# A PReLU gate's second projection by seven products for eight, its first projection in one PSUM bank, and weight forms written out once and read back

## The chip, the cores and the metric

The kernel runs on one core of one Trainium2 chip. A core has a matrix engine (TensorE, PE in the profile), a vector engine (VectorE, DVE), an activation engine (ScalarE, ACT), a general engine (GpSimd, POOL) and a queue engine that issues transfers (SyncE, SP). On-chip working memory is SBUF, with 128 partitions. Matmuls write into PSUM, which this kernel uses as eight banks of 512 float32 numbers for each partition; DVE and ACT read results from there. The metric is the device time of one execution in microseconds (us), as the median of several runs.

## The reference

Three stages follow one another; the output of one is the input of the next.

```python
A, Bm, C = softmax-like blocks of q, k and 32 landmark means        # 4 batches x 8 heads x 576 x 64
for _ in range(6): Z = 2 * Z - Z @ Bm @ Z                            # 32 x 32 pseudo-inverse
x = A @ Z @ C @ v                                                    # becomes 2304 x 512
h = x @ w_in;  x = (h * np.cos(h)) @ w_out                           # first gate, 512 -> 2048 -> 512
h = x @ w_in2; g = np.maximum(h, 0) + alpha * np.minimum(h, 0)       # second gate, 512 -> 2048
out = g @ w_out2                                                     # 2048 -> 512, float32, 2304 rows
```

The weights are given as float64. All else is float32.

## The kernel before, in words

**Precision.** A float32 matrix product is made of three matmuls. Each operand is split into a rounded high part and a low remainder (`hi` by ACT, `lo` by a subtraction on DVE or POOL), and the products hi·hi, hi·lo and lo·hi are added up in PSUM. The float64 weights are turned into float32 on the chip by three bit operations of DVE per 256 numbers (`convert`), and are written to DRAM tensors (`wi2d` and `wo2d` for the second gate) from which later stages load them.

**The second gate.** The change touches this gate alone, and what feeds it. Its 2304 tokens are worked off in chunks: chunks 0 to 3 of 512 tokens, chunk 4 of 256. Each chunk has eight steps, which I call ticks; a tick takes 256 of the 2048 hidden columns. Two ticks share a weight block (`sg`, four of them), and odd chunks take the blocks in reverse order, so that three block changes fall into each chunk. In the trace, ticks 1 to 8 of chunk 0 run from about 404 to 486 us, chunks 1 to 3 from 486 to 738 us, and chunk 4 to about 796 us.

**First projection of a tick** (`strassen`, L1341 to L1387). A product of two 2 x 2 block matrices is made by seven block products in place of eight, with sums of blocks on either side (the list `PRODUCTS`). A block product is six matmuls of 256 columns (two steps of 128 in depth, three matmuls each). The results are added up in four 256-wide quarters of two PSUM banks, `h` and `x`. Between the products, ACT or DVE copies a quarter out (L391, L393: `keep`), so that the next product can start there from zero, and at the end DVE adds both banks to the copies (L1383: `cross`, 512 elements each). The left operands, called forms here, are A11, A12, A21, A22 and the sums S1 to S4 of the weights, each split in hi and lo. S1 to S4 of all blocks are made once in chunk 0 and stay in SBUF (16 places `sr`); A11, A12 and A22 are loaded from `wi2d` (L1211) and split again for every block in every chunk (4 places `ss`). The right operands (B11, T1 and so on, made in `y_load`) belong to the chunk.

**PReLU and second projection of a tick.** DVE makes alpha·min(h, 0) (L1424) and adds max(h, 0) (L1427), for two halves of 512 elements. ACT makes the high part (L1429), DVE or POOL the low part (L396, a helper's line that many places share). Then come 24 matmuls of 512 columns (L1441): two halves by four groups of 128 tokens by three matmuls, adding up over the eight ticks in four PSUM banks `acc`. At a chunk's end the banks are copied out (L1461) and stored (L1467).

**What sets the order.** Every operation is named (`b25:9` is the ninth operation of the tick 25), and a long string `ORDER` lists the names in the order in which the program issues them; `Plan.go` (L313) walks it. An ending /V, /A or /G puts an operation on DVE, ACT or POOL where it may run on several. Each engine works its own operations off in that order. Buffers are places that rotate (`place`): an operation that fills one waits for the last reader of what was there before. Eight of the 16 blocks of w_out2 are converted under the first gate; the other eight in chunk 0 of the second gate (`late_wo2`, L1296).

## Time and profile before

| what | value |
|---|---|
| three runs, us | 801.34, 803.44, 803.97 |
| median, us | 803.44 |
| the profiled execution: its own time, us | 802.37 |
| its span in the trace, us | 800.6 |
| busy share of PE, DVE, ACT, POOL | 98%, 74%, 50%, 26% |
| granted clock of TensorE, mean over the span | 1.000 |
| data moved by DMA | 103.34 MB |

The span is the time between the first and the last instruction of the trace; the execution's own time is a little longer. A share of busy time is a mean over stages with different limits, so each stage has to be read by itself. Times in the trace count from the span's start.

### The profile page before, as it was taken

The numbers are of one execution on the slowest core, as the hardware profiler recorded it, in microseconds if no ns is written. First come the engines' busy times: TensorE is split into PE (matmuls) and PEld (weight loads), VectorE is DVE, ScalarE is ACT, GpSimd is POOL, SyncE is SP. The second block draws the span as 40 slices with busy tenths as digits, with TensorE's granted clock in tenths as the row PEclk, the third lists the DMA queues.
The fourth block names the chain that finished last, engine by engine and source line by source line (L and its number), as shares of the span: only waits on it lengthen the run. The fifth ranks groups of instructions, "written<-read, shape, count | busy, mean of one in ns | idle before, by whom it ended". The sixth has DMA issues, their size and how long they took to land.

```text
span 800.6 us, 16949 instructions
## 1 busy us (share of the span) xinstructions
PE 784.7 (98%) x6546; PEld 702.9 (88%) x6546; DVE 594.9 (74%) x1246; ACT 403.2 (50%) x919; POOL 209.0 (26%) x227
## 2 busy tenths in 40 slices
...
GB/s 259 259 296 138 120 191 187 151 203 179 223 167 264 119 265 112 237 166 109 198 93 122 89 97 93 80 27 41 53 79 40 54 38 95 47 46 33 83 84 26
DMA packets 106208, 103.34 MB, mean 129 GB/s; under 512 B 54160, under 2 KB 81296, under 8 KB 106128
## 3 DMA queue, kind: packets, MB, share of 16 engines
...
HBM read 79.96 MB, written 22.28 MB: 128 GB/s over the span
## 4 chain that ended last, share of the span: by engine, by line
PE 80%; DVE 8%; DMA 5%; ACT 3%; issue 2%; SPq 2%; POOL 1%; DVEq 0%; ACTq 0%
PE acc L1441 23%; PE acc L1071 20%; PE h L1360 11%; PE h L1046 10%; PE x L1360 8%; PE x L1002 2%; DVE m L396 2%; DMA m<-in_moe_w_in_dram 2%; DMA m<-in_moe_w_out_dram 1%; DMA m<-wi2d 1%; PE x L1405 1%; PE h L1405 1%; SPq L547 1%; PE x L939 1%; DMA wi2d<-m 1%
## 5 line engine op out<-in xcount | busy, mean ns | idle before, releaser
L396 POOL TENSOR_TENSOR m<-m,m 128x288 fp32r<-128x288 f32 (+4 forms) x156 | 150.5, 977 | 514.9 <-ACT m L1429 179.2
L1071 PE MATMUL acc<-m,m 128*128 128x288 f32 x1536 | 230.5, 297 | 0.4 <-DVE m L393 0.4
L1071 PEld LDWEIGHTS acc<-m,m 128*128 128x128 f32 x1536 | 210.5, 188 | 13.8 <-issue 7.9
L1441 PE MATMUL acc<-m,m 128*128 128x512 f32 x864 | 219.5, 394 | 1.0 <-ACT m L1429 0.9
L1441 PEld LDWEIGHTS acc<-m,m 128*128 128x128 f32 x864 | 154.0, 188 | 30.2 <-ACT m L1429 1.8
L396 DVE TENSOR_TENSOR m<-m,m 128x512 fp32r<-128x512 f32 (+4 forms) x244 | 146.0, 622 | 44.2 <-ACT m L1429 18.5
L1046 PE MATMUL h<-m,m 128*128 128x288 f32 x768 | 123.8, 298 | 0.9 <-DVE m L1056 0.4
L1046 PEld LDWEIGHTS h<-m,m 128*128 128x128 f32 x768 | 107.7, 188 | 7.1 <-DVE m L1056 3.2
L1360 PE MATMUL h<-m,m 128*128 128x256 f32 x660 | 93.3, 281 | 0.6 <-ACT m L391 0.6
L1429 ACT ACTIVATE m<-m 128x512 fp32r<-128x512 f32 (+1 forms) x80 | 46.1, 585 | 93.3 <-DVE m L1427 88.5
L1360 PEld LDWEIGHTS h<-m,m 128*128 128x128 f32 x660 | 87.9, 188 | 5.6 <-ACT m L391 1.0
L1055 ACT ACTIVATE m<-m,quarter 128x288 f32<-128x288 f32 x128 | 67.4, 533 | 37.2 <-DVE m L1053 36.6
L1360 PE MATMUL x<-m,m 128*128 128x256 f32 x576 | 81.6, 282 | 0.0
L1360 PEld LDWEIGHTS x<-m,m 128*128 128x128 f32 x576 | 76.5, 189 | 4.0
L1051 ACT ACTIVATE m<-h 128x288 int32<-128x288 f32 x128 | 51.6, 406 | 47.3 <-PE h L1046 46.6
L1056 DVE TENSOR_TENSOR m<-m,h 128x288 f32<-128x288 f32 x128 | 57.3, 451 | 22.6 <-ACT m L1055 18.1
L1053 DVE SCALAR_TENSOR_TENSOR m<-h,m 128x288 f32<-128x288 f32 x128 | 57.5, 451 | 18.0 <-ACT m L1051 17.0
L391 ACT ACTIVATE m<-h 128x256 f32<-128x256 f32 (+2 forms) x86 | 33.3, 391 | 73.3 <-PE h L1360 62.8
L1058 ACT ACTIVATE m<-m 128x288 fp32r<-128x288 f32 x128 | 54.4, 438 | 21.1 <-DVE m L1056 13.6
L1192 ACT ACTIVATE m<-m 128x512 fp32r<-128x512 f32 x68 | 41.5, 624 | 34.2 <-DMA m<-wi2d 14.2
L1427 DVE SCALAR_TENSOR_TENSOR m<-m,m 128x512 f32<-128x512 f32 x64 | 46.4, 741 | 0.8
L1383 DVE TENSOR_TENSOR m<-h,m 128x512 f32<-128x512 f32 x32 | 22.0, 686 | 32.7 <-ACT m L391 21.8
...
## 6 DMA issues: line engine op xcount, KB each, us to landing
...
m<-wi2d SPq DMA_DIRECT2D x56, 256.0 KB, 3.3
...
m<-w1d SPq DMA_DIRECT2D x32, 256.0 KB, 5.3
...
w1d<-m SPq DMA_DIRECT2D x16, 256.0 KB, 5.0
wi2d<-m SPq DMA_DIRECT2D x16, 256.0 KB, 3.8
```

Of the source, the lines that this page charges most:

```text
L396: ENG[e].tensor_tensor(o, a, b, op=ALU.subtract)
L1046: nc.tensor.matmul(out=hp.t[:, 0:CW], lhsT=w_[:, js], rhs=x[:, cs], start=(i == 0), stop=(i == 5))
L1051: op(act(CW, True), lambda e: nc.scalar.activation(k_.t, hp.t[:, 0:CW], AF.Copy, scale=INV2PI, bias=0.25), r=[hp], w=[k_], target=T + 0.8)
L1053: op(dve(CW), lambda e: nc.vector.scalar_tensor_tensor(u.t, hp.t[:, 0:CW], INV2PI, k_.t, op0=ALU.mult, op1=ALU.subtract), r=[hp, k_], w=[u])
L1055: op(act(CW), lambda e: nc.scalar.activation(u.t, u.t, AF.Sin, scale=2.0 * math.pi, bias=quarter), rw=[u], aset="sin")
L1056: op(dve(CW), lambda e: nc.vector.tensor_tensor(hc.t, u.t, hp.t[:, 0:CW], op=ALU.mult), r=[hp, u], w=[hc], target=T + 2.6)
L1058: op(act(CW), lambda e: nc.scalar.activation(gh.t, hc.t, AF.Copy), r=[hc], w=[gh, gl])
L1071: nc.tensor.matmul(out=yg[o].t[:, 0:CW], lhsT=w_.t[:, sl], rhs=x.t, start=(j == ja and i == 0), stop=(j == jb and i == 2),)
L1360: nc.tensor.matmul(out=rv(k), lhsT=a_.t[:, p, c2, js], rhs=b_.t[:, q_, c2, 0:hw], start=(first and c2 == 0 and i == 0), stop=(c2 == 1 and ...
L1427: op(dve(w), lambda e, m_=m_, hv=hv: nc.vector.scalar_tensor_tensor(m_.t[:, 0:w], hv(), 0.0, m_.t[:, 0:w], op0=ALU.max, op1=ALU.add), r=hr ...
L1429: op(act(w), lambda e, m_=m_, gh=gh: nc.scalar.activation(gh.t[:, 0:w], m_.t[:, 0:w], AF.Copy), r=[m_], w=[gh, gl])
L1441: nc.tensor.matmul(out=ya[n][t].t, lhsT=gv(x_), rhs=r_.t, start=(st and k == 0), stop=(en and k == 2))
```

## The change

**Second projection.** In chunks 1 to 3, `mtick` makes the second projection in the manner of the first: seven block products (`Y2`) of six matmuls of 256 columns each, in place of 24 matmuls of 512. For that the PReLU's result needs combinations (four sums of 256, L1556), and seven forms split in hi and lo (`form`); the output weights need theirs, made once per pair of blocks in chunk 1 (`t_make`, places `tt`). The seven products of all eight ticks add up in seven PSUM banks; at the chunk's end `y_out` adds these up and stores them. In chunk 4 the old form is used again, for which `t_drop` puts the plain halves of the output weights back.

**First projection.** Seven banks for the second projection leave one for the first. `narrow` makes its seven products in two quarters of this one bank, and each waits until the copy (L408, L411) or addition (L1487) before it has read the bank. Chunk 0 still uses `strassen` with two banks; in chunk 4 the two halves lie in one bank.

**Weight forms.** All forms of the first projection now share seven places. In chunk 0 each is made and written to a new DRAM tensor `wf2d` (28 writes of 512 KB, L1240). In chunks 1 to 3 all seven forms of a block are read back at each block change (`f_load`, L1266), with no splits; in chunk 4 three are, and A21 is made from `wi2d`.

**Conversion.** All 16 blocks of w_out2 are converted under the first gate (`LW` 8 for 4, one conversion in every 2 ticks of that stage for every 3), and `late_wo2` is gone. Buffers move in SBUF, and `ORDER` is written anew.

The diff, cut to its core (of `ORDER` nothing is shown; it differs over nearly its whole length):

```diff
-KN = dict(..., CD=3.0, LA=4, JG=8, VG=8, LW=4, LG=4)
+KN = dict(..., CD=2, LA=4, JG=8, VG=8, LW=8, LG=4)
...
+    wf2d = dram.tile([7, DFF // 512, P, 1024], F32, name="wf2d")
...
-    place["ss"] = (2, 4096, [z0 + 4096 * i for i in range(3)] + [at_raw + 16384])
-    place["sr"] = (2, 4096, [at_wi + 4096 * i for i in range(4)] + [at_raw + 4096 * i for i in range(4)]
-                   + [at_vb + 4096 * i for i in range(4)] + [at_a + 4 * 4 * S, at_a + 6 * 4 * S]
-                   + [at_g + 4096 * i for i in range(2)])
-    place["G"] = (2, 2048, [at_va + 2048 * i for i in range(8)])
+    place["sr"] = (2, 4096, [z0 + 4096 * i for i in range(3)] + [at_wi + 12288] + [at_raw + 4096 * i for i in range(3)])
+    place["G"] = (2, 2048, [at_va + 2048 * i for i in range(10)])
...
         def keep_(nm, src):
-            sw[nm, sg] = sb("ss" if nm in STREAM else "sr", [P, 2, 2, 256], F32R)
-            hl(sw[nm, sg], 2, lambda: src.t, [src], target)
+            t = sw[nm, sg] = sb("sr", [P, 2, 2, 256], F32R)
+            hl(t, 2, lambda: src.t, [src], target)
+            if first:
+                ap = wf2d[FORMS.index(nm), sg]
+                loads(1, lambda e: nc.sync.dma_start(out=ap, in_=f32(t.t.rearrange("p a c n -> p (a c n)"))), 1.3, ...)
...
+    def f_load(sg, target, names=FORMS):
+        for x, nm in enumerate(names):
+            t = sw[nm, sg] = sb("sr", [P, 2, 2, 256], F32R)
+            gates["q"] = [loads(
+                1, lambda e, t=t, ap=wf2d[FORMS.index(nm), sg]: nc.sync.dma_start(
+                    out=f32(t.t.rearrange("p a c n -> p (a c n)")), in_=ap), 1.3, ...)]
...
+    def narrow(n, i, sg, js, X, bank):
...
+        product(0, True, "A11", "B11")
+        product(1, False, "A12", "B21")
+        keep(sa, ka, 0, 0)
+        add(0, 1, sa, ka, 0)
+        product(0, False, "S2", "T2")
+        keep(sb_, kb, 0, 0)
+        product(0, False, "S3", "T3")
+        keep(sb_, kb, 1, 0)
+        product(1, True, "S1", "T1")
+        product(0, False, "A22", "T4")
+        add(2, 0, sb_, kb, 1, 2)
+        product(1, False, "S4", "B22")
+        add(1, 1, sb_, kb, 0)
...
+    def mtick(n, i, sg, jj):
...
+        if i == 0:
+            one[n] = psb("x"), g.buf(None)
+            ya[n] = [psb("acc") for _ in range(4)] + [psb("h") for _ in range(2)] + [psb("x")]
+        H, Hq = narrow(n, i, sg, js, *one[n])
...
+        form(0, ["A11"], lambda: m1.t[:, 0:256], [m1], 256)
...
+        comb(2, a21, a22, ms, ALU.add)
+        comb(0, lambda: H.t[:, 2], a11, [Hq[2], m1], ALU.subtract)
+        comb(1, a11, a21, [m1], ALU.subtract)
+        comb(3, a12, lambda: H.t[:, 0], [m2, Hq[0]], ALU.subtract)
+        form(1, ["A12", "A22"], lambda: m2.t, [m2], 512)
+        form(2, ["S2", "S3"], lambda: flat(H.t[:, 0:2]), Hq[0:2], 512)
+        form(4, ["S1", "S4"], lambda: flat(H.t[:, 2:4]), Hq[2:4], 512)
...
-            btick(n, i, sg, jj)
+            (mtick if 0 < n < len(chunks) - 1 else btick)(n, i, sg, jj)
```

Where the instructions stand now is seen at three places, in the order in which the engine issues them (line, operation, what it writes and reads by buffer names, size, and how many in a row).

PE in the second tick of chunk 3, before. `h`, `x` and `acc` are PSUM banks; L1360 and L1475 are the first projection, L1441 and L1585 the second.

```order
L1360 MATMUL h<-m_4843,m_4443 128x256 x6
L1360 MATMUL h<-m_4443,m_5454 128x256 x6
L1360 MATMUL x<-m_4843,m_4443 128x256 x6
L1441 MATMUL acc<-m_1787,m_608 128x512 x3
L1360 MATMUL x<-m_4894,m_1371 128x256 x6
L1441 MATMUL acc<-m_1140,m_813 128x512 x6
L1441 MATMUL acc<-m_1140,m_814 128x512 x3
L1360 MATMUL h<-m_4894,m_731 128x256 x6
L1360 MATMUL x<-m_4894,m_731 128x256 x6
L1441 MATMUL acc<-m_1140,m_814 128x512 x3
L1360 MATMUL h<-m_4946,m_1411 128x256 x6
```

The rows of PE at the same place with the change:

```order
L1475 MATMUL x<-m_4466 128x256 x6
L1475 MATMUL x<-m_5171,m_4466 128x256 x6
L1585 MATMUL h<-m_5073,m_594 128x256 x6
L1585 MATMUL acc<-m_1130,m_616 128x256 x6
L1475 MATMUL x<-m_5196,m_4466 128x256 x6
L1585 MATMUL acc<-m_5073,m_616 128x256 x6
L1475 MATMUL x<-m_5196,m_4768 128x256 x6
L1585 MATMUL acc<-m_1130,m_615 128x256 x6
L1475 MATMUL x<-m_5196,m_5073 128x256 x6
L1475 MATMUL x<-m_5378,m_5073 128x256 x6
L1585 MATMUL h<-m_1130,m_615 128x256 x6
L1475 MATMUL x<-m_5171,m_5073 128x256 x6
```

In the rows of after, one or two products of the second projection stand between products of the first that must wait for each other; before, products of the first projection stand in runs of up to three, in two banks, and the second projection's matmuls, twice as wide, in fewer places.

DVE in the fourth tick of chunk 2, before. L1383, L1487: additions out of PSUM. L393, L411: copies out of it. L1424, L1427, L1527, L1530: PReLU. L1556: combinations. L396, L414: low parts.

```order
L1383 TENSOR_TENSOR m_644<-h,m_644 128x2x256
L393 COPY m_697<-h 128x256
L1383 TENSOR_TENSOR m_644<-x,m_697 128x512
L1424 TENSOR_SCALAR m_559<-m_644,alpha_sb 128x512
L1424 TENSOR_SCALAR m_633<-m_644,alpha_sb 128x512
L1427 SCALAR_TENSOR_TENSOR m_559<-m_644,m_559 128x512
L396 TENSOR_TENSOR m_813<-m_559,m_813 128x512
L1427 SCALAR_TENSOR_TENSOR m_633<-m_644,m_633 128x512
L393 COPY m_644<-x 128x256
L393 COPY m_697<-h 128x256
L396 TENSOR_TENSOR m_814<-m_633,m_814 128x512
```

The rows of DVE at the same place with the change:

```order
L1487 TENSOR_TENSOR m_658<-x,m_658 128x256
L1530 SCALAR_TENSOR_TENSOR m_273<-m_576,m_273 128x512
L411 COPY m_658<-x 128x256
L1530 SCALAR_TENSOR_TENSOR m_345<-m_576,m_345 128x512
L1556 TENSOR_TENSOR m_576<-m_345,m_273 128x256
L1556 TENSOR_TENSOR m_576<-m_576,m_345 128x256
L414 TENSOR_TENSOR m_616<-m_345,m_616 128x256
L1556 TENSOR_TENSOR m_576<-m_273,m_576 128x256
L414 TENSOR_TENSOR m_819<-m_576,m_616 128x512
L1487 TENSOR_TENSOR m_658<-x,m_658 128x512
L1487 TENSOR_TENSOR m_658<-x,m_658 128x256
```

More of DVE's instructions now are of 256 elements, and between the additions that free the one bank stand parts of the PReLU and of the forms.

SP at the change from chunk 0 to chunk 1, before. `wi2d`, `wf2d` and `wo2d` are the weights in DRAM, `out_dram` is the result.

```order
L1211 DMA m_4431<-wi2d 128x2x256
L1211 DMA m_4433<-wi2d 128x2x256
L1211 DMA m_4438<-wi2d 128x2x256
L1211 DMA m_4496<-wi2d 128x2x256
L1211 DMA m_4431<-wi2d 128x2x256
L1467 DMA out_dram<-m_1336 64x512 x2
L1211 DMA m_4433<-wi2d 128x2x256
L1467 DMA out_dram<-m_1392 64x512 x2
```

The rows of SP at the same place with the change:

```order
L1371 DMA m_1329<-wo2d 128x512
L1266 DMA m_4466<-wf2d 128x1024
L1371 DMA m_1177<-wo2d 128x512
L1266 DMA m_4466<-wf2d 128x1024 x2
L1266 DMA m_4768<-wf2d 128x1024
L1266 DMA m_5073<-wf2d 128x1024 x3
L1706 DMA out_dram<-m_1393 64x512 x2
L1706 DMA out_dram<-m_1327 64x512 x2
L1371 DMA m_1177<-wo2d 128x512
L1706 DMA out_dram<-m_1329 64x512 x2
```

The queue's loads of 256 KB from `wi2d` have become refills of 512 KB from `wf2d`, and the loads for `t_make` (L1371) stand among them and the stores.

## Rows read from the trace of the kernel before

**Rows 1.** The page's first part: busy us (share of the span) and instructions.

```profile
PE 784.7 (98%) x6546; PEld 702.9 (88%) x6546; DVE 594.9 (74%) x1246; ACT 403.2 (50%) x919; POOL 209.0 (26%) x227
```

**Rows 2.** Stretches: busy us of each engine (instructions), PE clock, DMA share, GB/s.

```profile
core 0: us, PE busy (x) PEld busy (x) DVE busy (x) ACT busy (x) POOL busy (x), PEclk, DMA share, GB/s
40.00:530.00 490.00, 484.09 (x4303) 440.73 (x4295) 416.08 (x898) 297.03 (x681) 159.27 (x172) 1.00 0.56 160
404.50:486.00 81.50, 80.90 (x532) 73.77 (x531) 76.99 (x146) 38.80 (x84) 12.77 (x12) 1.00 0.32 100
486.00:737.70 251.70, 251.70 (x1578) 226.42 (x1577) 152.68 (x260) 87.74 (x202) 45.72 (x46) 1.00 0.18 54
737.70:796.50 58.80, 57.74 (x341) 49.89 (x339) 30.37 (x59) 15.87 (x34) 8.81 (x10) 1.00 0.21 68
```

**Rows 3.** PE in time: start us, us, line, operation, out<-in, count.

```profile
450.39 5.73 PE L1441 MATMUL acc<-m,m 128*128 128x512 f32 x24
455.97 0.40 PE L1360 MATMUL h<-m,m 128*128 128x256 f32 x2
...
593.14 0.88 PE L1360 MATMUL h<-m,m 128*128 128x256 f32 x6
...
594.59 2.27 PE L1360 MATMUL h<-m,m 128*128 128x256 f32 x18
596.70 0.62 PE L1441 MATMUL acc<-m,m 128*128 128x512 f32 x2
```

**Rows 4.** The page's fifth part: the first projection's weight loads (busy us, mean ns).

```profile
L1360 PEld LDWEIGHTS h<-m,m 128*128 128x128 f32 x660 | 87.9, 188 | 5.6 <-ACT m L391 1.0
```

**Rows 5.** ACT in time: the copy of a quarter.

```profile
594.06 0.38 ACT L391 ACTIVATE m<-h 128x256 f32<-128x256 f32 x1 [0.34 <-PE h L1360]
```

**Rows 6.** Groups by shape, 400 to 800 us, and line 1383 (ns min/median/max).

```profile
L393 DVE COPY m<-h 128x256 f32<-128x256 f32 x20 | 8.4, 420 | 14.8 <-PE h L1360 14.8
L1383 DVE TENSOR_TENSOR m<-h,m 128x512 f32<-128x512 f32 x32 | 22.0, 686 | 32.7 <-ACT m L391 21.8 <-PE h L1360 6.7 <-issue 4.1
L396 POOL TENSOR_TENSOR m<-m,m 128x512 fp32r<-128x512 f32 x20 | 26.7, 1336 | 209.2 <-ACT m L1429 135.9 <-ACT m L1192 48.6 <-DVE m L1312 18.7
L396 POOL TENSOR_TENSOR m<-m,m 128x256 fp32r<-128x256 f32 x33 | 26.4, 812 | 87.8 <-ACT m L1429 43.3 <-ACT m L1282 38.3 <-PE h L1405 6.1
...
L1383 DVE TENSOR_TENSOR m<-h,m x32: 674/686/693, 410.8 to 737.9; 128x512 f32<-128x512 f32 x32
```

**Rows 7.** DVE in time.

```profile
626.69 1.29 DVE L1427 SCALAR_TENSOR_TENSOR m<-m,m 128x512 f32<-128x512 f32 x2
...
630.05 2.40 DVE L396 TENSOR_TENSOR m<-m,m 128x512 fp32r<-128x512 f32 x2 [0.65 <-ACT m L1192]
...
636.17 1.84 DVE L1427 SCALAR_TENSOR_TENSOR m<-m,m 128x512 f32<-128x512 f32 x2
...
658.32 0.41 DVE L396 TENSOR_TENSOR m<-m,m 128x256 fp32r<-128x256 f32 x1
658.65 0.68 DVE L1427 SCALAR_TENSOR_TENSOR m<-m,m 128x512 f32<-128x512 f32 x1
659.26 0.47 DVE L1424 TENSOR_SCALAR m<-m,alpha_sb 128x512 f32<-128x512 f32 x1
```

**Rows 8.** POOL in time, beside the rows above.

```profile
630.62 1.29 POOL L396 TENSOR_TENSOR m<-m,m 128x512 fp32r<-128x512 f32 x1 [1.13 <-ACT m L1429]
...
636.35 1.11 POOL L396 TENSOR_TENSOR m<-m,m 128x256 f32<-128x256 f32 x1 [4.45 <-DMA m<-y1d]
637.42 1.18 POOL L396 TENSOR_TENSOR m<-m 128x256 f32<-128x256 f32 x1
```

**Rows 9.** The page's sixth part: transfers (count, KB each, us from issue to landing).

```profile
m<-wi2d SPq DMA_DIRECT2D x56, 256.0 KB, 3.3
wi2d<-m SPq DMA_DIRECT2D x16, 256.0 KB, 3.8
```

**Rows 10.** Two more stretches, as in rows 2, and the page's count of packets.

```profile
0.00:60.00 60.00, 52.26 (x831) 39.29 (x832) 45.12 (x126) 37.21 (x82) 13.69 (x17) 1.00 0.99 271
8.00:12.00 4.00, 3.17 (x57) 2.59 (x57) 2.37 (x5) 1.78 (x6) 0.00 (x0) 1.00 1.03 398
DMA packets 106208, 103.34 MB, mean 129 GB/s; under 512 B 54160, under 2 KB 81296, under 8 KB 106128
```

741 lines of the change are left out of this document (465 added, 276 removed).

## The prediction

> **What bounds the kernel now.** I read the busy shares first, then the busy times by stretch, then the order of the matmuls in time. PE is busy 784.7 of 800.6 us [rows 1]. By stretch it is fuller still: in chunks 1 to 3 of the second gate, 486.0 to 737.7 us, it is busy 251.70 of 251.70 us, while DVE is busy 152.68, ACT 87.74, POOL 45.72, and the DMA engines 0.18 of the time [rows 2]. Only work taken off PE can shorten that stretch. The granted clock is 1.00 in every one of these stretches [rows 2], the 2.4 GHz level, and nothing here would lower it.
>
> That PE is busy does not yet say that it issues as fast as it can, so I take start to start. Twenty-four matmuls of 512 columns run from 450.39 to 455.97, 0.2325 us each; eighteen of 256 columns run from 594.59 to 596.70, 0.1172 us each [rows 3]. Half the columns cost half the time; the smaller matmul pays next to nothing extra. A tick of chunks 1 to 3 is 42 matmuls of 256 and 24 of 512: 42 x 0.1172 + 24 x 0.2325 = 10.50 us. Twenty-four ticks make 252.1 us, and the stretch took 251.7: it is PE at its pace, with no gap worth a name.
>
> **What the change takes off PE.** In 24 ticks the second projection becomes 7 products of 6 matmuls of 256 columns, 42 x 0.1172 = 4.92 us, where 24 x 0.2325 = 5.58 stood. That is 0.66 a tick and **15.8 us** in all. A tick is then 84 x 0.1172 = 9.84 us at PE's pace.
>
> The Trainium skill (TensorE: Matmul & The Clock Gate, Part 3, The mechanism) says that a weight load overlaps with running matmuls only where their row groups differ, and here they never do. By it the 18 more weight loads a tick would stand open. The eighteen matmuls above each have a load of their own, of 188 ns [rows 4], and still start every 117 ns; the trace disagrees, so the rule is only the last rival below.
>
> **What it adds, term by term.**
>
> *Handoffs in one bank: 5.2 us.* The first projection now adds up in one bank, and a product must wait until the bank has been read. A product that started at 593.14 was read from 594.06 on (0.92 us later) for 0.38 us by ACT [rows 5], and the product that needed its place started at 594.59 [rows 3]: 1.45 us from start to start, of which 0.15 is the way back to PE. In the order of the changed kernel PE does second-projection products meanwhile (0.703 us each): per tick 2, 1, 1, 2, 1 of them in the five gaps. A gap with one product covers 1.41 us. The two gaps behind an ACT copy lose 0.04 each; the one behind a DVE addition of 256, taken as 0.42 like DVE's copy from PSUM [rows 6], needs 0.92 + 0.42 + 0.15 = 1.49 and loses 0.08. Gaps with two cover 2.11, against 1.87 for copy and addition and 1.76 for the addition of 512 (0.686 [rows 6]). That is 0.16 a tick, 3.8 us. In four ticks (1 to 3 of chunk 2, 2 of chunk 3) the gap of the 512 addition has one product and lacks 0.35: 1.4 us.
>
> *DVE in crowded ticks: 4.5 us, from 3 to 10.* Counted in the order over chunks 1 to 3, DVE goes from some 51 instructions of 256 elements, 156 of 512 and 46 minima to 223, 143 and 51; POOL from 27 of 256 and 14 of 512 to 86 and 25. Back to back DVE needs 0.33 us for 256 and 0.61 for 512 [rows 7], a minimum some 0.45: 223 x 0.33 + 143 x 0.61 + 51 x 0.45 = 184 us. POOL becomes 86 x 0.812 + 25 x 1.336 = 103 us [rows 6]. The two disturb each other: two subtractions at 630.05 took 2.40 us, about 1.1 more than their 1.29 back to back, while POOL ran 1.29; two instructions at 636.17 took 1.84, 0.55 more, beside 1.66 of POOL [rows 7, 8]. So a us of POOL costs DVE 0.33 to 0.86. Additions out of PSUM are spared (674 to 693 ns in all 32 [rows 6]). I take 0.45 and let 0.7 of POOL's time fall on DVE's other work: 103 x 0.7 x 0.45 = 32 us, DVE 216 of the 236 us that 24 ticks last. It fits as a sum but not tick by tick. DVE runs in order, so what stands between the last additions of two ticks must pass in one tick. Adding it up so, four ticks go over PE's time: tick 5 of chunk 1 by 1.1 us, ticks 8 of chunk 1 and 1 of chunk 2 by 0.5 each, tick 3 of chunk 2 by 0.9; tick 8 of chunk 2 comes to 0.25 over. That is 3.3, the lower end. DVE also idles in each tick between its last two additions, while PE does two products and one more. Walking through tick 6 of chunk 1 with these durations, a tick without excess, its 512 addition comes 0.5 late, because ACT's split of the tick before stands behind two copies. A quarter of such lateness in every tick would give 10, the upper end; I take 4.5, nearer the lower because in a light tick (2 of chunk 3) everything came out in time.
>
> *Chunk 0: 2 us, from 0 to 6.* All first-projection weight forms now live in 7 places instead of 20, so a new block's form waits for the last product of the old one and for the landing of its copy to DRAM (writes of half the size land after 3.8 us [rows 9]). Then comes ACT's split and DVE's or POOL's, 0.6 + 0.7 to 1.3 us. From release to need PE has nine to eleven products, some 7 us. The first forms fit; the last ones depend on DVE, which is busy 76.99 of 81.50 us there now [rows 2] and loses 48 conversions of 256 elements (16 us at 0.33). Three changes of block at 0 to 2 us each.
>
> *At nothing.* The 8 blocks of output weights that were converted in chunk 0 are converted under the first gate: 24 more DVE instructions, 15 us, and eight loads; PE is busy 484.09 of 490 there and DVE 416.08 [rows 2], so PE hides them (0 to 2 us if not). Seven refills of 0.524 MB for a new block replace ACT and DVE work: 3.67 MB at 398 GB/s [rows 10] last 9.2 us, within the 9.84 us between a form's last product and its next; landing takes 3.3 us for half the size [rows 9]. Behind a waiting refill on SP stand the next refills, the loads for the next chunk and the stores of the result, none needed within a tick. The seven sums are read out at a chunk's end in the order in which they are next written, a tick ahead each. Chunk 4 makes one form a block where it made four, where PE is busy 57.74 of 58.80 us [rows 2]: 0 to 1 us of gain, taken as 0.
>
> **Sum.** -15.8 + 5.2 + 4.5 + 2 = -4.1 us. The profiled execution took 802.37 us for a span of 800.6; it becomes 798.3. The median of the three runs is 803.44, so **799.3 us** there. The ends of the terms (handoffs kept) give -15.8 + 5.2 + 3 + 0 = -7.6, so 795.8, and -15.8 + 5.2 + 10 + 6 = +5.4, so 808.8.
>
> **Rivals.**
>
> *The cover holds.* For it: in chunk 0 DVE is busy 76.99 of 81.50 us and PE still 80.90 [rows 2], so a crowded DVE need not hold PE up. Then only some 3 us of handoffs are left: -12.8, **790.6 us**. Against it: there, four bank quarters wait separately, and now one bank does.
>
> *DVE becomes the bound, and the kernel is slower.* At the 0.86 of the worse pair, DVE needs 184 + 103 x 0.7 x 0.86 = 246 us, 10.25 a tick; with about 0.6 idle before its last addition, 10.85, or 260 us for the stretch against 252: +8, and +2 in chunk 0, **813.5 us**. It decides from about 0.6 us of DVE per us of POOL, where a tick passes today's 10.50. The Trainium skill (SBUF - State Buffer, Who interferes with whom) says that a DVE instruction with two SBUF inputs and a GpSimd instruction that reads SBUF exclude each other, the loser waiting for the whole instruction, while one with at most one SBUF input is spared. The trace agrees about the additions out of PSUM. A whole POOL us lost each time would make it 184 + 72 = 256 us, 10.7 a tick before any idling; the pair at 636.17 shows less.
>
> *The refills come late.* At the 271 GB/s of the first 60 us [rows 10] a block takes 13.5 us, 3.7 more than a tick, in nine changes: +33, about **832 us**. Against it: half of the run's packets are under 512 B [rows 10], and the refills move rows of 4 KB.
>
> *Weight loads stand open.* 24 x 18 x 0.188 = 81 us more: **869 us**.
>
> **Chances.** Forecast 0.53, cover holds 0.18, DVE the bound 0.22, refills 0.05, weight loads 0.02. What a measurement tells from no change is about 0.3%, 2.4 us: 801.0 to 805.8 is the same. Of the forecast's own 796 to 809 I put 0.55 below that, 0.33 in it, 0.12 above. Faster: 0.18 + 0.29 = 0.47. Same: 0.18. Slower: 0.06 + 0.29 = 0.35. For 8 in 10 the range takes most of the cover case and of the DVE case: 791 to 814.
>
> **What would show it.** Right: matmuls of the second projection starting every 0.117 us; ticks of 10.0 to 10.3 us in chunks 1 to 3, with PE's waits behind ACT's copies and DVE's additions, under 0.5 us each and most in ticks 1 to 3 of chunk 2; chunk 0 within 3 us of before. Wrong: DVE near 10 us busy in every tick, its subtractions well above 0.69 us (the DVE rival); PE waiting for landings at every second tick (refills); no wait above 0.1 us (cover); or a loss outside the second gate, which no term here prices.

## The result and the profile after

| | median, us | runs, us | ratio to before, 95% interval |
|---|---|---|---|
| before | 803.02 | 800.73 to 805.19 (12 runs) | |
| after | 806.85 | 804.70 to 809.72 (12 runs) | 1.0052 [1.0035, 1.0070] |

The change costs 0.5%. The forecast was a gain of 4 us, so the time lies within the stated range of 791 to 814 us, but on the other side of no change. The profiled execution of after took 806.84 us, with a span of 805.1 (before: 800.6), at a granted clock of 1.00. The next lines answer to rows 1, 9 and 2; first the page's busy times and its transfers.

```profile
PE 780.2 (97%) x6978; PEld 717.5 (89%) x6978; DVE 653.0 (81%) x1364; ACT 410.6 (51%) x934; POOL 294.4 (37%) x310
...
m<-wf2d SPq DMA_DIRECT2D x72, 512.0 KB, 5.3
wf2d<-m SPq DMA_DIRECT2D x28, 512.0 KB, 5.0
```

By stretch (busy us of each engine and instructions, clock, DMA share, GB/s), for chunk 0, chunks 1 to 3 and chunk 4 of the second gate:

```profile
404.50:486.00 81.50, 80.17 (x551) 74.67 (x550) 71.72 (x125) 43.24 (x94) 29.86 (x27) 1.00 0.76 262
486.00:740.00 254.00, 249.49 (x1977) 241.54 (x1976) 209.16 (x396) 96.33 (x220) 100.42 (x101) 1.00 0.50 170
740.00:801.00 61.00, 58.02 (x392) 52.62 (x390) 32.34 (x69) 14.69 (x35) 18.32 (x20) 1.00 0.37 121
```

In chunks 1 to 3 PE is no longer busy throughout [rows 2]: 4.5 of 254 us are empty, and time is lost also where PE shows as busy (next section). DVE has gone from 152.68 in 251.70 us to 209.16 in 254, POOL from 45.72 to 100.42. In chunk 0 PE has about the same work as before, DVE 5 us less, POOL 17 more, and the writes and reads of the forms raise the traffic from 100 to 262 GB/s. In chunk 4 3.0 us of 61 are empty, where 1.1 of 58.80 were. The refills land 5.3 us after their issue, in the middle, within the 9.84 us that the prediction gave them.

### The profile page after: what moved, and what is told of

It is laid out like the page before. It is cut to its first block, busy times and chain, and to the rows that moved or that the text cites. A ratio compares the mean times of both kernels' runs of the same rounds, so it can differ in the third digit from the quotient of the medians.

```text
span 805.1 us, 18263 instructions
## 1 busy us (share of the span) xinstructions
PE 780.2 (97%) x6978; PEld 717.5 (89%) x6978; DVE 653.0 (81%) x1364; ACT 410.6 (51%) x934; POOL 294.4 (37%) x310
## 5 line engine op out<-in xcount | busy, mean ns | idle before, releaser
L414 POOL TENSOR_TENSOR m<-m,m 128x288 fp32r<-128x288 f32 (+4 forms) x197 | 202.3, 1037 | 364.3 <-ACT m L1074 166.1
L1087 PEld LDWEIGHTS acc<-m,m 128*128 128x128 f32 x1536 | 210.7, 188 | 14.8 <-issue 6.6
L414 DVE TENSOR_TENSOR m<-m,m 128x512 fp32r<-128x512 f32 (+4 forms) x255 | 148.3, 602 | 19.4 <-ACT m L1543 5.6
L1475 PE MATMUL x<-m,m 128*128 128x256 f32 x864 | 126.7, 286 | 3.2 <-DVE m L1487 2.6
L1062 PEld LDWEIGHTS h<-m,m 128*128 128x128 f32 x768 | 107.7, 188 | 10.7 <-DVE m L1072 8.0
L1475 PEld LDWEIGHTS x<-m,m 128*128 128x128 f32 x864 | 110.6, 188 | 7.4 <-DVE m L1487 4.8
L409 ACT ACTIVATE m<-x 128x256 f32<-128x256 f32 (+5 forms) x91 | 35.4, 395 | 94.4 <-PE x L1475 82.2
L1585 PE MATMUL acc<-m,m 128*128 128x256 f32 x568 | 80.9, 280 | 0.0
L1072 DVE TENSOR_TENSOR m<-m,h 128x288 f32<-128x288 f32 x128 | 57.3, 451 | 25.2 <-ACT m L1071 22.2
L1543 ACT ACTIVATE m<-m 128x512 fp32r<-128x512 f32 (+1 forms) x96 | 53.0, 574 | 44.6 <-DVE m L1556 16.9
L1585 PEld LDWEIGHTS acc<-m,m 128*128 128x128 f32 x568 | 73.1, 189 | 0.2
L1680 PE MATMUL acc<-m,m 128*128 128x512 f32 x288 | 72.6, 394 | 0.0
L1069 DVE SCALAR_TENSOR_TENSOR m<-h,m 128x288 f32<-128x288 f32 x128 | 57.2, 450 | 13.2 <-ACT m L1067 11.9
L1680 PEld LDWEIGHTS acc<-m,m 128*128 128x128 f32 x288 | 51.6, 188 | 9.2
L1487 DVE TENSOR_TENSOR m<-x,m 128x256 f32<-128x256 f32 (+1 forms) x72 | 36.8, 511 | 28.3 <-PE x L1475 22.9
L571 DVE SCALAR_TENSOR_TENSOR m<-m,m 128x512 int32<-128x512 int32 x64 | 46.7, 733 | 0.4
L573 DVE SCALAR_TENSOR_TENSOR m<-m,m 128x512 int32<-128x512 int32 x64 | 46.0, 724 | 0.2
```

The source lines that it names most:

```text
L414: ENG[e].tensor_tensor(o, a, b, op=ALU.subtract)
L1062: nc.tensor.matmul(out=hp.t[:, 0:CW], lhsT=w_[:, js], rhs=x[:, cs], start=(i == 0), stop=(i == 5))
L1069: op(dve(CW), lambda e: nc.vector.scalar_tensor_tensor(u.t, hp.t[:, 0:CW], INV2PI, k_.t, op0=ALU.mult, op1=ALU.subtract), r=[hp, k_], w=[u])
L1072: op(dve(CW), lambda e: nc.vector.tensor_tensor(hc.t, u.t, hp.t[:, 0:CW], op=ALU.mult), r=[hp, u], w=[hc], target=T + 2.6)
L1087: nc.tensor.matmul(out=yg[o].t[:, 0:CW], lhsT=w_.t[:, sl], rhs=x.t, start=(j == ja and i == 0), stop=(j == jb and i == 2),)
L1475: nc.tensor.matmul(out=rv(r), lhsT=a_.t[:, p, c2, js], rhs=b_.t[:, q_, c2], start=(first and c2 == 0 and y == 0), stop=(c2 == 1 and y == 2 ...
```

## Where the time went

PE's busy time says little here, because a record's end is modelled. So I weighed every matmul at the pace that matmuls of its width keep (0.1172 us for 256 columns and 0.2325 for 512, both from [rows 3], and 0.1328 for 288, from starts in the first gate), and compared for both traces the time that is left at a point with the work that is left. The difference between the traces by stage:

| stage | us, after against before |
|---|---|
| matmul work that fell away in chunks 1 to 3 | -15.8 |
| first gate (to about 404 us) | +4.8 |
| chunk 0 | +0.5 |
| chunks 1 to 3, waits beyond before's | +12.9 |
| chunk 4 | +2.1 |
| sum | +4.5 (the spans: 805.1 - 800.6) |

**The matmuls became as cheap as thought.** PE in time, in a run of second-projection products of six matmuls each:

```profile
752.14 0.88 PE L1585 MATMUL h<-m,m 128*128 128x256 f32 x6
752.86 0.88 PE L1585 MATMUL x<-m,m 128*128 128x256 f32 x6
```

They start 0.72 us apart, six matmuls at 0.12 each. The weight loads do not stand open.

**The first gate lost 4.8 us, nearly all in one stretch.** I compare the start of the n-th of the 1536 matmuls of the first gate's second projection with its start in before:

```
n-th matmul (start in before)   205 (109.2)  481 (170.1)  865 (273.2)  1536 (421.8)
after                              -0.6         +4.1         +4.1         +5.5
```

It falls between 109 and 170 us (between these places the two orders mix the projection's matmuls with others differently, and the difference swings by up to 2 us). There PE now waits, which it did not before: in the waits of PE from 100 to 170 us (us in total, times, longest) before has no row, and after has this one:

```profile
PE h L1062 <- DVE m L1072: 2.7, 6, 0.9
```

The timeline of after at one of the six shows what stands ahead of DVE's L1072, which the matmuls wait for:

```profile
131.84 0.43 DVE L569 TENSOR_SCALAR m<-m 128x512 int32<-128x512 int32 x1 [0.97 <-DMA m<-in_moe_w_in_dram]
132.19 0.69 DVE L571 SCALAR_TENSOR_TENSOR m<-m,m 128x512 int32<-128x512 int32 x1
132.79 1.05 DVE L414 TENSOR_TENSOR m<-m,m 128x512 fp32r<-128x512 f32 x2
133.76 0.45 DVE L1069 SCALAR_TENSOR_TENSOR m<-h,m 128x288 f32<-128x288 f32 x1
134.13 0.44 DVE L1072 TENSOR_TENSOR m<-m,h 128x288 f32<-128x288 f32 x1
...
134.63 1.07 PE L1062 MATMUL h<-m,m 128*128 128x288 f32 x6 [0.90 <-DVE m L1072]
```

DVE stood idle for 0.97 us until a weight block had landed, worked at its conversion (L569, L571) and at low parts (L414), and only then did L1069 and L1072, for which PE waited 0.90 us.

**Chunks 1 to 3 lose in two kinds of delay.** I took the time from one matmul's start to the next's, less the pace of the first. In before, none is late by over 0.2 us there, and eleven by 0.05 to 0.2 (1.1 us together). In after, 11 are late by over 0.2 us (6.3 us together) and 77 by 0.05 to 0.2 (7.1 us). Together 13.4, 12.3 more than before, which is nearly all of the 12.9.

The short ones. 71 of the 77 stand behind the first matmul of a first-projection product, 0.090 us each on average, and 56 of these behind the three products whose gap holds one product of the other projection: A11·B11 (21), S1·T1 (19), S3·T3 (16). In the timeline of after one looks so (PEld is the weight load):

```profile
503.44 0.41 DVE L1487 TENSOR_TENSOR m<-x,m 128x256 f32<-128x256 f32 x1
...
503.90 0.77 PEld L1475 LDWEIGHTS x<-m,m 128*128 128x128 f32 x6 [0.49 <-DVE m L1487]
503.90 0.97 PE L1475 MATMUL x<-m,m 128*128 128x256 f32 x6
504.60 1.24 PEld L1680 LDWEIGHTS acc<-m,m 128*128 128x128 f32 x6
504.71 1.55 PE L1680 MATMUL acc<-m,m 128*128 128x512 f32 x6
```

DVE's addition ended at 503.85, and at 503.90 PE started both the load and the matmul. The product takes 0.81 us to the next one's start, where six matmuls need 0.70. The product behind it, which waits for nothing, has its load 0.11 us ahead of its matmul. The Trainium skill (TensorE: Matmul & The Clock Gate, Step-by-step: what each phase is for) says that PE pulls weight loads ahead of running matmuls; the trace agrees for the product that waits for nothing (0.11 ahead), and shows that the one that had to wait got no such lead. That is what a short delay consists of. In the 82 first-projection products of chunks 1 to 3 whose second matmul starts over 0.02 us late, the lead of the first weight load (0 to 0.09) and the delay add up to 0.10 to 0.12 us each time. Of the 71, 57 start within 0.02 us of PE's pace; the bank was read in time for the matmul and too late for its weight load.

Of the 11 long ones, 9 (5.0 us) stand in front of a product that waits for the bank's readers, most of them additions that DVE comes to late; one waits for a form's low part (0.8) and one for a refill (0.5). The waits of PE from 486 to 745 us:

```profile
PE x L1475 <- DVE m L1487: 3.2, 6, 0.9
PE h L1585 <- DVE m L414: 0.6, 1, 0.6
PE x L1475 <- DMA m<-wf2d: 0.4, 1, 0.4
```

The first tick of chunk 3, in time:

```profile
660.06 0.87 PE L1475 MATMUL x<-m,m 128*128 128x256 f32 x6
...
661.03 0.39 ACT L409 ACTIVATE m<-x 128x256 f32<-128x256 f32 x1 [1.25 <-PE x L1475]
...
661.48 1.35 DVE L414 TENSOR_TENSOR m<-m,m 128x512 fp32r<-128x512 f32 x3
662.76 0.41 DVE L1487 TENSOR_TENSOR m<-x,m 128x256 f32<-128x256 f32 x1
...
663.22 0.98 PE L1475 MATMUL x<-m,m 128*128 128x256 f32 x6 [0.93 <-DVE m L1487]
```

The product of 660.06 was copied out by ACT from 661.03 to 661.42, as in [rows 5]. DVE's addition could have followed then; low parts stood ahead of it in DVE's queue, so it began at 662.76, and PE lost 0.93 us.

**Chunk 4** has its two halves in one bank now, and waits for the PReLU to have read it (waits of PE from 738 to 802 us in after, then from 737 to 801 in before):

```profile
PE x L1644 <- DVE m L1666: 2.9, 3, 1.6
```

```profile
PE acc L1441 <- ACT m L1429: 0.9, 2, 0.7
```

## The experiments

Three questions: what slowed the first gate, what the delays in chunks 1 to 3 are made of, and whether chunk 4 can be mended. Where ratios are given they are to the kernel before.

### The first gate: the conversions or the order?

The eight blocks that are now converted here, left out; their loads read another block instead:

```diff
+SKIP = {f"c{i}" for i in range(56, 64)}
-            if e:
+            if e and o.key[0] not in SKIP:
-   ... in_=wo2d[j]
+   ... in_=wo2d[kept(j)]
```

> The changed kernel without the eight conversions of output weights that it added under the first gate: their loads, 24 DVE instructions and writes are left out, and the blocks that they would have made are read from the blocks made before them. Theory A (order): these conversions stand at 330 to 380 us, behind the stretch in which the time is lost, so 0 to 1.5 us less, 805.4 to 807. Theory B (the added DVE work): some 4.8 us less, 802.

Measured: 806.61 us, 1.0045 [1.0025, 1.0066]. The first gate's loss stayed. The added conversions are not its cause.

The order of before up to about 270 us of the first gate; the operations that had moved ahead stand behind it. Of the string the first names:

```diff
-u0:1 w:10 u0:2 w:4 c0:1 u1:1 w:2 w:3
+u0:1 u0:4 w:10 w:4 w:2 w:3
...
```

> The changed kernel with one edit: from the start to tick 78 of the first gate (about 270 us) the operations are issued in the order of the kernel before; all else, the added conversions among it, is the change's. Theory A (the changed kernel loses about 4.8 us there because its re-planned order puts DVE's steps of the first gate behind work that waits): 802 us, 801 to 803.5, against 806.9 for the change, and the first gate's last matmul about 4 us earlier. Theory B (the loss comes from the 24 added DVE instructions of the eight conversions moved under the first gate): they are still there, so no gain, 806 to 808.

Measured: 825.18 us, 1.0271 [1.024, 1.0303]. The matmuls of the table above kept before's pace up to the seam (+0.6 at the 481st, 0.0 at the 865th), and at the seam PE waited twice for DVE, which had the operations held back to do (PE's waits from 240 to 340 us, and one of the two in time):

```profile
PE h L1066 <- DVE m L1076: 18.5, 2, 9.7
```

```profile
295.66 1.81 PE L1066 MATMUL h<-m,m 128*128 128x288 f32 x6 [8.82 <-DVE m L1076]
```

PE stood from 286.8 us on, and from 290.5 to 311.0 us the granted clock was at 0.5, the 1.2 GHz level; the six matmuls above take 1.81 us where six of the same size took 1.07 at 134.63. By engine, as in rows 2:

```profile
290.00:311.00 21.00, 5.68 (x22) 5.33 (x23) 9.80 (x20) 2.32 (x6) 0.00 (x0) 0.51 0.71 223
```

The time is the seam's; what is behind it says nothing. Up to it, the run speaks for the order. So the next one has the order of before up to about 130 us only, where nothing is held back:

```diff
-u0:1 w:10 u0:2 w:4 c0:1 u1:1 w:2 w:3
+u0:1 u0:4 w:10 w:4 w:2 w:3
...
```

> The changed kernel, issued in the order of the kernel before up to tick 43 of the first gate (about 130 us) and from there in the change's own, with no operation held back at the seam. Theory A (the re-planned order between 113 and 159 us loses 4 to 6 us): the first gate's matmuls keep to the times of the kernel before, and the whole is 4 to 5 us faster than the change, 802.2, 801 to 803.5. Theory B (the loss there is paid later anyway, since DVE's work under the first gate has only been shifted): 805 to 808.

Measured: 804.89 us, 1.0026 [1.0007, 1.0044]. The 481st matmul starts 0.2 us after before's, where after is 4.1 late; the 1536th 2.0 after, where after is 5.5. PE has no wait from 100 to 170 us. Of the profiles taken, the eleven with the changed order lose 3.0 to 4.7 us between the 205th and the 481st matmul, and the seven with the old one 0.0. That the order costs this is shown. Not all of it comes back: from the 205th matmul to the last, the eleven lose 3.5 to 6.0 us (5.2 on average), and the six with the old order to 130 us still 1.8 to 4.7 (2.8). These 2.4 us fit the 2.0 of the medians, whose intervals allow some 0 to 4; the forecast of 802.2 had taken it that all comes back.

### Chunks 1 to 3: what are the delays made of?

**The bank's readers read something else.** Copies and additions read a weight tile in SBUF, so no product waits for them (the first projection's results are then not used):

```diff
-   copy(e, d.t[:, x], rv(r)), r=[bank], ...
+   copy(e, d.t[:, x], f32(wo2[0][0].t[:, 0:256])), ...
-   H.t[:, x:x + z], rv(r, z) ... r=[bank, kd[y]]
+   H.t[:, x:x + z], f32(wo2[0][0].t[:, 0:256 * z]) ... r=[kd[y]]
```

> The changed kernel, but in chunks 1 to 3 the copies and additions of the first projection read a fixed weight tile in SBUF in place of the PSUM bank (what the bank holds is not read), so that no product waits for a reader of the bank; the counts of instructions stay. Theory A (the waits of the one bank and what DVE adds to them cost 13 us in chunks 1 to 3, 7 of them as delays of about 0.1 us behind the first matmul of a product): 13 us less, 794 us, 791 to 796, and no matmul start to start of over 0.2 us in the ticks. Theory B (PE's pace: the 18 more weight loads a tick, or the smaller matmuls): the delays stay, 803 to 807.

Measured: 806.49 us, 1.0032 [1.0013, 1.0052]. The short delays fell from 77 (7.1 us) to 15 (1.5 us), so they do belong to the bank. But the additions now have two operands in SBUF, and beside POOL they became slower; DVE's busy time in the stretch rose from 209 to 229 us. The longer waits grew from 6.3 to 11.6 us, on forms that came late. The run changed two things at once and weighs neither.

**No handoffs in ticks 4 to 8 of each chunk.** There (15 of 24 ticks) all seven products are written to a bank of the second projection and wait for no reader; the copies and additions read the first bank in their old form and wait for no product (so both projections' results are lost there):

```diff
+            Z = ya[n][0] if i > 2 else X
-   out=rv(r), ...
+   out=Z.t[:, 256 * r:256 * r + 256], ...
-   rw=[bank], ...
+   rw=[g.buf(None) if i > 2 else bank], ...
```

> The changed kernel, but in ticks 4 to 8 of chunks 1 to 3 (15 of 24) the first projection's products are written to a bank of the second projection, while the copies and additions still read the one bank: the same instructions on all engines, and no wait between products and their readers. (What is computed there is not the gate's.) Theory A (the handoffs cost about 0.1 us behind three products a tick): the delays of 0.05 to 0.2 us fall from some 77 to some 30, the longer ones, most of which are in ticks 1 to 3, stay; 4 to 5.5 us faster than the change, 802, 801 to 803. Theory B (DVE's load decides): the waits move to the second projection's forms, 806 to 808.

Measured: 802.58 us, 1.0003 [0.9986, 1.0019], 4.3 us under after. Short delays fell to 41 (3.9 us); in the 15 ticks themselves from 4.2 to 0.7 us, and 12 of the 15 have none, where in after each has some. Its profiled execution is the slowest of its runs (807.12; they go from 801.0), with 2.5 us of waits for refills (0.4 in after), so the medians are to be read here and the trace only for the delays.

**Less work for DVE.** The low parts of the forms are left out and the high parts used in their place:

```diff
-   sub(e, lo(), src(), f32(hi()))
+   None
-   for G in (hi(), lo())
+   for G in (hi(), hi())
```

> The changed kernel, but in chunks 1 to 3 the low parts of the second projection's forms are not made (4 subtractions a tick fewer on DVE and POOL); the matmuls read the high part in their place, so PE's work stays. Theory A (of the 13 us, 6 come from a DVE that is late and 7 from the bank's own handoffs, which no lighter DVE removes): 6 us less, 801, 799 to 802.5, and the delays of 0.1 us behind a product's first matmul remain, some 70. Theory B (all of it is DVE's load): 12 us less, 795. Theory C (the chain through the bank alone): 806 to 807.

Measured: 802.09 us, 0.9983 [0.9965, 1.0001], 4.8 under after. DVE's busy time fell to 166 us, the long delays to 8 (3.3 us), the short ones to 64 (5.7 us): 4.3 us less in all, near the 4.8 of the medians. The stretch, and behind it PE's wait for additions, half of after's:

```profile
486.00:740.00 254.00, 251.94 (x2013) 245.10 (x2013) 166.28 (x342) 98.23 (x226) 64.14 (x76) 1.00 0.50 170
```

```profile
PE x L1475 <- DVE m L1487: 1.6, 4, 0.7
```

**Less of POOL.** POOL's share of the forms and combinations is left out, DVE's stays:

```diff
-   sub(e, lo(), src(), f32(hi()))
+   sub(e, lo(), src(), f32(hi())) if e == "DVE" else None
-   ENG[e].tensor_tensor(H.t[:, x], a(), b(), op=alu)
+   ENG[e].tensor_tensor(H.t[:, x], a(), b(), op=alu) if e == "DVE" else None
```

> The changed kernel, but in chunks 1 to 3 the low parts and combinations of the second projection that the order puts on POOL are left out (the matmuls read what stood in those places); DVE keeps all its instructions. Theory A (DVE's additions come late because DVE's instructions on SBUF wait for POOL's: 29 us over their usual lengths there, and a minimum that takes 1.32 us beside a POOL subtraction in place of 0.48): DVE's excess falls from 29 to some 12 us, and the time by 2 to 4 us, 804, 803 to 805. Theory B (DVE's own load makes it late): no gain, 806 to 808.

Measured: 806.79 us, 1.0038 [1.0023, 1.0052]. The long delays stayed (10, 6.4 us), though POOL fell from 100 to 35 us in the stretch and DVE from 209 to 197. The disturbance by POOL is real and does not set the time. The stretch:

```profile
486.00:740.00 254.00, 249.17 (x1985) 241.95 (x1984) 196.80 (x396) 96.29 (x221) 35.41 (x38) 1.00 0.50 170
```

**One hop more for DVE.** In every tick the first addition comes one product later, behind S2·T2's place in the program (and, in the order, behind the next copy):

```diff
-        add(0, 1, sa, ka, 0)
         product(0, False, "S2", "T2")
+        add(0, 1, sa, ka, 0)
```

> The changed kernel with one edit: in chunks 1 to 3 the first addition out of the one bank (A12 B21 onto the copy) comes a product later, beside the copy after S2 T2, so that S2 T2 waits for ACT's copy alone and the chain through the bank is about 0.4 us shorter in each tick. Theory A (the chain through the bank is as long as a tick, and late additions go straight into the time): 2 to 4 us faster than the change, 804, 803 to 805.5. Theory B (DVE's load decides, wherever its additions stand): 806 to 808.

Measured: 829.84 us, 1.0329 [1.0315, 1.0342], 23 over after. No engine has more work (DVE is busy 208 us in the stretch); PE waits 14.5 us for additions, and DVE stands 26.0 us behind ACT's copies, where it stood 4.1 in after. The waits from 486 to 770 us:

```profile
DVE m L1487 <- ACT m L409: 26.0, 15, 2.5
...
PE x L1475 <- DVE m L1487: 14.5, 25, 2.6
```

The same row in after:

```profile
DVE m L1487 <- ACT m L409: 4.1, 8, 1.4
```

Both theories missed, and the trace shows why. The product S3·T3 now waits for the copy and the addition, and came over 0.2 us late in 23 of 24 ticks (14.6 of the run's 26.6 us of long delays). In one of them, in time:

```profile
633.97 0.87 PE L1585 MATMUL acc<-m,m 128*128 128x256 f32 x6
634.16 0.42 DVE L411 COPY m<-x 128x256 f32<-128x256 f32 x1 [0.48 <-PE x L1475]
634.51 0.41 DVE L1487 TENSOR_TENSOR m<-x,m 128x256 f32<-128x256 f32 x1
634.98 0.95 PE L1475 MATMUL x<-m,m 128*128 128x256 f32 x6
```

The addition went out of a gap with two products into a gap with one. By the prediction's own figures, copy and addition need 1.87 us there and have 1.41, which lacks 0.46; the median of the 23 delays is 0.45. Another 3.0 us are matmuls at a granted clock of 0.5 (the 1.2 GHz level), in two stretches of 3.4 us, each within 1.3 us of the end of a wait of PE of 2.1 and 2.7 us. So the run does not weigh the length of the chain against DVE's load; it shows what a gap without cover costs.

**No refills.** The reads from `wf2d` in chunks 1 to 4 are left out, and old forms are used:

```diff
-   nc.sync.dma_start(out=f32(t.t ...), in_=ap)
+   None
```

> The changed kernel without the refills: the first projection's forms aren't read back in chunks 1 to 4, and the products read what chunk 0 left in those places. Theory A (refills are hidden but for the landing that PE waited 0.53 us for in the trace): 0.5 to 1.5 us faster than the change, 806, 805 to 806.5. Theory B (seven refills of 512 KB at each change of block hold PE up more than its own waits show, through the loads and stores behind them on the queue): 4 us or more, below 803.

Measured: 806.57 us, 1.0043 [1.0028, 1.0058]. PE waits for additions as in after (3.2 us in 6 waits), so the refills, and what their traffic could do to others, cost nothing that a median shows.

**More cover.** 48 single matmuls of the second projection moved into the gaps that lack a little. A product may now be issued in two parts; five of its six matmuls before the waiting product, one after the next:

```diff
-b17:34 b20:5
+b17:34#5 b20:5 b17:34#z
```

> The changed kernel with 48 small moves on PE alone in chunks 1 to 3: where a first-projection product waits for the one bank behind a single second-projection product, one matmul of a neighbouring second-projection product (of six) is issued in that gap, so that seven matmuls stand there in place of six, and eleven where twelve stood. Theory A (the delays of about 0.1 us behind a product's first matmul arise because the gap lacks 0.04 to 0.1 us of cover, which 0.12 us more takes away): of 77 such delays some 40 go, and the time falls by 3 to 4 us against the change, 803.5, 802.5 to 805. Theory B (a wait on a bank costs its 0.1 us however much stands before it): no gain, 806 to 808.

Measured: 808.73 us, 1.0066 [1.0041, 1.0091], not under after. The short delays fell from 77 to 50, at the three products named above from 56 to 20; but the long ones went from 11 to 17 and from 6.3 to 9.8 us. What was saved at the short delays (2.4 us) was lost again at long ones (3.5), refills among them. PE's two largest waits in the stretch were 3.2 and 0.4 us in after and are here:

```profile
PE x L1483 <- DVE m L1495: 4.5, 7, 1.1
PE x L1483 <- DMA m<-wf2d: 1.3, 3, 0.6
```

**The minimum on ACT.** Takes one DVE instruction in each half of the PReLU away, and puts one hop to ACT and back in its place:

```diff
-   nc.vector.tensor_scalar(m_.t, hv(), 0.0, alpha_sb[:, j:j + 1], op0=ALU.min, op1=ALU.mult)
+   nc.scalar.activation(m_.t, hv(), AF.Relu, scale=neg_sb[:, j:j + 1])
-   op0=ALU.max, op1=ALU.add
+   op0=ALU.max, op1=ALU.subtract
```

> The changed kernel, but in chunks 1 to 3 the PReLU's minimum is made on ACT, as Relu(-alpha h), which DVE then subtracts from max(h, 0): 48 instructions of 0.48 us and more leave DVE, and ACT, busy 96 of 254 us there, takes 48 of some 0.6. What is computed stays the same. Theory A (DVE's own load delays its reads of the bank and the forms): DVE is busy some 180 us in place of 209, the longer waits shrink from 6 to some 3 us, and the time by 2 to 4 us, 804, 803 to 805. Theory B (the reads wait for the chain through the bank, whoever works beside it; ACT's copies out of the bank now stand behind minima): 806 to 809.

Measured: 822.58 us, 1.0241 [1.0214, 1.0268], 16 over after, though DVE is busy for 20 us less. The stretch, which has become longer, and DVE's largest wait for ACT in it:

```profile
486.00:760.00 274.00, 259.99 (x2024) 250.86 (x2023) 189.62 (x352) 127.21 (x270) 99.80 (x102) 0.98 0.47 160
```

```profile
DVE m L1533 <- ACT m L1530: 24.5, 17, 3.0
```

While DVE waits for ACT's minimum, the next addition out of the bank stands behind it in DVE's queue. The long delays became 22 (17.6 us, 11.3 more than in after). The short ones became 114 (11.1 us), but 42 of these (4.4 us) are matmuls at a granted clock of 0.5, the 1.2 GHz level, which lasted 3.4 us three times, each time within 1 us of the end of a wait of PE of 2.0 to 2.8 us; the other 72 (6.7 us) are about as many as in after. The second of the three, with 20 matmuls where 1.00 has room for some 31:

```profile
569.00:572.60 3.60, 3.60 (x20) 3.60 (x20) 1.63 (x3) 0.42 (x1) 1.18 (x1) 0.53 0.54 203
```

So of the 16 us some 11 are the hop and some 4 the clock.

### Chunk 4, and the mended parts together

Two banks in chunk 4 from its second tick on (in the order, one product stands a little later):

```diff
+            X2 = psb("h") if i else X
-                D = g.buf(None)
+                D, Z = g.buf(None), X2 if x else X
-   out=X.t[:, 128 * x:128 * x + w], ... hold=[X]
+   out=Z.t[:, 128 * x:128 * x + w], ... hold=[Z]
```

> The changed kernel, but from the second tick of chunk 4 on the two halves of the first projection lie in two PSUM banks, as before the change. Theory A (three waits of PE for the PReLU's reads, 3.4 us in all, against 1.5 in the kernel before, come from the shared bank): 1.5 to 2.5 us faster than the change, 804.8. Theory B (they come from the order at the end, in which less other work is left): no gain, 806 to 808.

Measured: 802.85 us, 0.9997 [0.9978, 1.0016]. PE's waits in chunk 4 are before's again, in the row that answers to after's 2.9:

```profile
PE x L1645 <- DVE m L1667: 0.9, 1, 0.9
```

By the rows that is 2 us; by the medians 4.0, where the two intervals together allow some 2 to 7.

The old order to 130 us and the two banks together, with no other edit:

```diff
-u0:1 w:10 u0:2 w:4 c0:1 u1:1 w:2 w:3
+u0:1 u0:4 w:10 w:4 w:2 w:3
...
+            X2 = psb("h") if i else X
```

> The changed kernel with both of the repairs that gained alone: the order of the kernel before up to tick 43 of the first gate, and two banks for the first projection in chunk 4. If the two gains (2.1 and 4.0 us by the medians, 4 and 2.5 us by the waits in the traces) add up, 801, 800 to 802.5, which is 0.1 to 0.4% faster than the kernel before; if they are the same gain seen twice, 802.5 to 804.5.

Measured: 804.41 us, 1.0007 [0.9988, 1.0026]. By the medians the two parts do not add up (2.0 and 4.0 alone, 2.4 here); by the ratios to before they gain 0.26% and 0.55% alone and 0.45% here. The intervals are too wide to make anything of it.

Ten additions and copies out of the bank moved ahead of other DVE work, on top of that; one of the ten:

```diff
-b24:25 b25:16 b25:13
+b24:25 b25:13 b25:16
```

> The kernel of the run before with ten swaps on DVE in chunks 0 to 3: at the places where the trace shows a read of the one bank late and PE waiting for it, that read is issued one or two instructions earlier. No instruction is added or left out. Theory A (DVE's lateness at these few places goes straight into the time): 2 to 3 us less than without the swaps, 798.5, 797.5 to 800. Theory B (what is moved behind the read comes late in its turn): within 1 us of the run before.

Measured: 803.49 us, 0.9996 [0.998, 1.0012], 0.9 us under the run before: no gain that is clear of noise.

The moved matmuls on top of that:

```diff
-b9:30 b11:5
+b9:30#5 b11:5 b9:30#z
```

> The version with the old order in front, two banks in chunk 4 and the ten swaps on DVE, and the same moves of single matmuls on PE. Theory A: 3 to 4 us less than without the moves (803.5), 800, 798.5 to 801.5, which is 0.3 to 0.6% faster than the kernel before. Theory B: as without them, 802.5 to 804.5.

Measured: 801.80 us, 0.9987 [0.9966, 1.0007]: 5 us under the change, and the fastest of those that leave nothing out; that it is faster than before is not shown. With DVE's additions earlier, the moved matmuls take 1.7 us off, which the intervals do not tell from nothing; alone they made it no faster.

The minimum on ACT once more, on the last two versions:

```diff
+   nc.scalar.activation(m_.t, hv(), AF.Relu, scale=neg_sb[:, j:j + 1])
```

> The version with the old order in front, two banks in chunk 4 and the ten swaps (803.5 us, 0.9996 of before), and the minimum on ACT. Theory A: 800.5, 799 to 802. Theory B: 803 to 806.

> The same with the moves of single matmuls on PE (801.8 us without ACT's minima, 0.9987 of before). Theory A: DVE's lateness and the lack of cover are two separate losses, and with both smaller 798.5, 797 to 800.5. Theory B (the one chain through bank, DVE and ACT keeps its length): 801 to 804.

Measured: 814.71 us, 1.0137 [1.011, 1.0163], and 813.85 us, 1.0123 [1.0101, 1.0146]: 11 and 12 us over the same versions with the minimum on DVE. Here the granted clock was 1.00 throughout chunks 1 to 3, and the long delays are 16.9 and 15.7 us, against 5.9 and 8.5 without the hop. Theory A and Theory B both missed, by 8 us and more.

## Why the forecast was wrong

The forecast's sum was -4.1 and the spans differ by +4.5. The 8.6 us between them, by the table above, are 4.8 in the first gate, 3.2 in chunks 1 to 3, 2.1 in chunk 4, less 1.5 in chunk 0.

**"At nothing", the first gate: the step that failed most.** The conversions were priced at 0 to 2 us because PE is busy there anyway [rows 2]. They cost nothing that shows (the run without them is no faster). What I did not price is that the order was written anew there too. A stretch in which PE is full was taken to hide what happens on DVE; but DVE has an operation in the loop of every tick of that gate, and six of these came late, by up to 0.9 us. What the runs showed in place of 0 is 4.8 us. The prediction itself named a loss outside the second gate as what would make it wrong, since no term covered one. The old order in that stretch avoids the loss there, and about half of it lasts to the end (2.0 us by the medians).

**Handoffs, 5.2 us: right in kind, too small.** The part for gaps that lack a few hundredths was 3.8 us; the short delays are 7.1 (1.1 in before). At the three gaps that were meant they are 4.9: I took latency less cover, 0.04 to 0.08 for each, and measured are 0.08 to 0.09 where one occurs, in 56 of 72 places. Another 1.3 us, 13 delays, stand at the gaps with two products, which I had taken as free. It was wrong to think that a wait of 0.04 costs 0.04: the bank must be read a further 0.11 us ahead, so that the weight load has its lead, or the second matmul starts late, as at 503.90 above. The other part, 1.4 us, stands with the next term.

**DVE in crowded ticks, 4.5 us: size right, places half right.** With the 1.4 us of handoffs in crowded ticks it was 5.9; measured are 6.3 less 0.5 for a refill. DVE's busy time was foretold as 216 us and is 209; its excess beside POOL as 32 and is 29. Of the crowded ticks foretold, tick 5 of chunk 1 (delays of both kinds: 0.9 us) and ticks 1 (1.5) and 3 (1.5) of chunk 2 are among the worst, while tick 8 loses 0.4 in chunk 1 and 0.3 in chunk 2; missed were tick 2 of chunk 1 (1.0) and ticks 1 (1.3) and 2 (1.7) of chunk 3. Summing the work between the last additions of two ticks finds some crowded ticks; it does not see an addition in the middle of a tick that stands behind low parts, as at 662.76.

**Gap by gap, or one chain?** The prediction walked gap by gap. The seven products also form one chain through the bank, and with the prediction's own durations it is 0.70 + 1.87 + 1.45 + 1.45 + 0.70 + 1.76 + 1.49 = 9.42 us from a tick's first product to the next tick's, with the delays at five handoffs some 9.9. That is no less than PE's 9.84, and by this sum alone there would be no reserve. The trace of after shows one. At the gaps with two products the bank had been free for 0.24 us or more when the product started, in 16 of 24 ticks at S2·T2 and in 17 at S4·B22 (medians 0.29 and 0.43). In tick 7 of chunk 2, in time:

```profile
645.10 1.53 PE L1585 MATMUL h<-m,m 128*128 128x256 f32 x12
645.49 0.68 DVE L1487 TENSOR_TENSOR m<-x,m 128x512 f32<-128x512 f32 x1
646.46 0.88 PE L1475 MATMUL x<-m,m 128*128 128x256 f32 x6
```

The addition ended at 646.17, and PE came to S4·B22 at 646.46, when it was through with the two products before. At the three gaps with one product the bank became free 0.02 to 0.14 us ahead in 67 of 71 cases. So the step from gap to gap was right, and a late addition by DVE finds some 0.3 to 0.4 us of reserve at two gaps of a tick and next to none at three. The runs fit this. An addition moved from a gap with two products to one with a single product costs 23 us with no more work, 14.6 of delay at that gap alone; a hop to ACT and back costs 11 to 12 with less work for DVE; fewer instructions in DVE's queue give 4.8 back, and no handoffs in 15 ticks 4.3, each near what its trace takes off the delays it was meant for (4.3 and 3.5). Why the moved matmuls brought nothing alone does not follow from it. That the two kinds of delay make up the loss in these chunks is read from starts in the trace; no run has the two-bank chain with all else as in after. POOL's disturbance, which the DVE rival rested on, does not decide.

**Chunk 4, taken as 0: 2.1 us.** I counted the forms it saves and not that its halves share a bank; a two-bank version has before's waits again.

**Right:** 15.8 us less for PE; chunk 0 within 3 us of before (0.5, where 2 was forecast); most quiet ticks at 10.0 to 10.2 us; refills that are mostly in time (the rival at 832 us fell); weight loads under matmuls (869 fell). The cover did not hold, so 790.6 fell too. The DVE rival at 813.5 expected ticks of 10.85 us throughout; only some are as long, with single late additions. Not right was that no wait would be over 0.5 us; the longest is 0.9.

**What stays open.** What refill waits cost in a usual run (0.4 us in after's profile, 1.3 to 2.5 in others, while the run without refills is no faster); where the first gate loses the 2.8 us that remain with the old order in front; how much of chunk 4's gain is real beyond 2 us; and why more cover did not pay alone.
